# Order of the first loads, split product, shared copies and a halved last tile in a fused linear-attention and mixer kernel

## Chip, cores, metric

One core of a Trainium2 chip. The metric is the device time of one execution in microseconds (us).

In the lines of the profile PE is TensorE (PEld its loads of weights), DVE VectorE, ACT ScalarE, POOL GpSimd and SP SyncE; a "bank" is a buffer in PSUM, into which PE writes. A line of the chain (the work that ended last, followed back step by step) gives its start in us from the start of the span, its length in us, and what ran; L363 is line 363 of that kernel's file. The granted clock is the share of full speed that TensorE was given, 1.00 being all of it.

## The reference

Linear attention with phi(x) = elu(x) + 1, then an MLP mixer over tokens and channels, for 8 batches, 8 heads, 576 tokens, head size 64:

```python
q_p, k_p = phi(q), phi(k)
kv = einsum('bhsd,bhse->bhde', k_p, v);  z = sum(k_p, axis=2)
x = einsum('bhsd,bhde->bhse', q_p, kv) / (einsum('bhsd,bhd->bhs', q_p, z)[..., None] + 1e-6)
# x laid out as (batch, 576, 512)
h = relu(x.T @ w_tok1) @ w_tok2;   u = x + h.T        # token mixing, 256 wide
out = u + relu(u @ w_ch1) @ w_ch2                     # channel mixing, 1536 wide
```

## The kernel before

Matmuls run in bf16. The channel matmuls of a batch are interleaved with the attention of a later one, so PE is busy nearly all the time. Only the first batch has nothing to hide behind; it has code of its own, in two groups of four heads ("group 0" and "group 1", index `c`). For the first batch phi(k) is held as two terms that are summed in the product: `kr` = relu(k) and `kp` = min(exp(k), 1).

```python
for c, nms in enumerate(("kq", "qk")):        # SyncE's queue: k0, q0, q1, k1
    for nm in nms:
        load(nm, 0, c)
...
for c in range(2):                            # GpSimd's queue: v of group 0, v of group 1
    load_v0(c)
...
warm(27)                                      # matmuls on the identity, result unused
...
ksum_first(0, act)                            # sums of k: 18 matmuls, copies on ScalarE
warm(2)
kv_first(0, act)                              # product k by v: 36 matmuls, 64 rows each
...
nd_first(0)                                   # denominators, numerators
...
ksum_first(1, act); kv_first(1, act)
num_first(0, 0, R); num_first(0, R, 1)
nd_first(1)
mm1_first(...)                                # token matmul 1
mm2_first(0, [0, 1]); mm2_first(0, [2, 3])    # token matmul 2 in tiles of 64 columns,
mm2_first(1, [0, 1])                          #   each with u = x + h on VectorE
utr_first([0, 1], act)                        # transposes of u, copy of 128x1024 on ScalarE
mm2_first(1, [2, 3])
mm3(0, 0, range(0, 2))                        # channel matmul 1, first column
utr_first([2], act); utr_first([3], dve)
for mc in range(1, 3): mm3(0, mc, range(0, 2))   # "second column" below: mc = 1
```

The 64 rows of each batch that do not fill a tile of 128 ("tail rows") are transposed in pairs by a DMA into `uTt`, and `m3t` are the channel matmuls on them. The last batch ends with one output tile whose 12 matmuls of 512 columns are followed by one add and two stores:

```python
def mm4_end(p, t):
    ...
    nc.vector.tensor_tensor(out=o, in0=ps, in1=u[b][:, r, :], op=ALU.add)
    ... # the two halves of the partitions are stored from SyncE and from ScalarE
for n in range(2, B):
    ...
    big = m3(n) + m3t + m4(p, [4, 5, 6, 7, 8] if n + 1 < B else [8, 4, 5, 6, 7])
```

## Time and profile before

| | before |
|---|---|
| median time, 3 runs | 267.51 us (267.28 to 267.62) |
| span of the profiled execution | 265.8 us |
| PE busy | 256.6 us, 97% |
| second column of channel matmuls starts | 23.17 us |
| PE's last matmuls end (chain) | 261.13 us |
| last store lands | 264.51 us |

The time is the span plus about 1.8 us. The profile's lines of the opening and of the end stand in the prediction. "Second column" is the mark at which the opening is over: from there on PE has almost no gap. It is read from the timeline as the start of the second run of channel matmuls (the first has two matmuls only). Where PE does not wait, starts of matmuls in the timeline are some 0.04 to 0.2 us ahead of the same matmuls in the chain, which counts from when the result before them was complete.

### The profile page before, as it was taken

The page shows a single profiled execution, that of the slowest core. Times are in us where ns is not written, and L with a number is a line of the kernel's source. Part 1 is how long each engine was busy: PE and PEld are TensorE (multiplying, and loading weights), DVE is VectorE, ACT ScalarE, POOL GpSimd, SP SyncE. Part 2 cuts the span into 40 slices and gives each one's busy share as a digit, 9 for nine tenths or more (in the row PEclk, how much of TensorE's full clock was granted, in tenths as well). Part 3 has the DMA queues.
Part 4 walks back from the last instruction along what each step waited for, and adds up shares of the span by engine and source line. Part 5 has one row for each costly group of instructions (what it writes and reads, how often), then busy time and mean ns, then how long its engine had stood idle before and what let it go on. Part 6 is the DMA issues. An engine that isn't in the chain of part 4 may idle for free.

```text
span 265.8 us, 5142 instructions
## 1 busy us (share of the span) xinstructions
PE 256.6 (97%) x2107; PEld 134.1 (50%) x2107; DVE 158.2 (60%) x311; ACT 132.8 (50%) x200; POOL 33.4 (13%) x54
## 2 busy tenths in 40 slices
PE   7999989999999999999999999999999999999992
PEld 2684445554744454455554554455564554444641
DVE  5764967966839686948684286939684272320121
ACT  5645768268464358525771358435870363036300
POOL 9720300120002300030001300030001300000000
PEclk9999999999999999999999999999999999999999
DMA  7999999399406995899999990671074500730043
GB/s 260 246 203 280 373 214 399 133 191 402 168 2 125 191 383 201 108 239 369 285 411 210 258 409 32 143 171 36 2 135 116 118 2 0 162 94 2 0 118 79
DMA packets 49927, 48.34 MB, mean 182 GB/s; under 512 B 30256, under 2 KB 35248, under 8 KB 49904
## 3 DMA queue, kind: packets, MB, share of 16 engines
q1 hardware_dynamic: 41824, 35.53, 46.8%
q0 software_dynamic: 7440, 11.44, 20.4%
q10 hardware_dynamic: 640, 1.05, 1.2%
q8 instruction: 16, 0.26, 0.4%
q14 instruction: 7, 0.06, 0.1%
HBM read 35.85 MB, written 9.44 MB: 170 GB/s over the span
## 4 chain that ended last, share of the span: by engine, by line
PE 87%; DMA 4%; DVE 3%; ACT 2%; issue 1%; POOL 0%; ACTq 0%; POOLq 0%
PE h_ps L501 34%; PE c_ps L475 27%; PE a_ps L248 5%; PE h_ps L261 5%; DMA uTt<-ut 4%; PE c_ps L489 4%; PE bank L545 3%; PE nd_ps L210 3%; PE kv_ps L169 2%; ACT e L125 1%; PE bank L363 1%; PE bank L413 1%; DVE e L139 1%; DVE vs L151 1%; PE bank L385 1%
## 5 line engine op out<-in xcount | busy, mean ns | idle before, releaser
L482 ACT ACTIVATE cr<-c_ps 128x512 bf16<-128x512 f32 x91 | 53.5, 598 | 78.0 <-PE c_ps L475 77.8
L475 PE MATMUL c_ps<-uT,wc 128*128 128x512 bf16 x384 | 91.5, 379 | 0.4 <-ACT uT L444 0.4
L501 PE MATMUL h_ps<-wc,cr 128*128 128x512 bf16 x384 | 87.4, 379 | 0.0
L501 PEld LDWEIGHTS <-cr 128*128 128x128 bf16 x384 | 37.1, 98 | 43.0
L475 PEld LDWEIGHTS <-wc 128*128 128x128 bf16 x384 | 35.7, 98 | 36.5 <-issue 1.0
L518 DVE TENSOR_TENSOR o_sb<-h_ps,u 128x512 f32<-128x512 f32 x32 | 21.8, 688 | 28.0 <-PE h_ps L501 27.9
L523 POOL DMA_DIRECT2D out_dram<-o_sb x24 | 14.9, 627 | 154.1 <-DVE o_sb L518 154.1
L222 DVE TENSOR_TENSOR x<-nd_ps,den 128x512 bf16<-128x512 f32 (+1 forms) x42 | 25.3, 602 | 1.4
L139 DVE TENSOR_SCALAR e<-e 128x1152 bf16<-128x1152 bf16 x30 | 13.9, 463 | 12.7 <-ACT e L125 12.6
L125 ACT ACTIVATE e<-k_raw 128x1152 bf16<-128x1152 f32 x16 | 18.7, 1170 | 2.3 <-DMA k_raw<-in_k_dram 2.3
L125 ACT ACTIVATE e<-q_raw 128x1152 bf16<-128x1152 f32 x16 | 18.5, 1161 | 1.6 <-DMA q_raw<-in_q_dram 1.4
L273 DVE TENSOR_TENSOR u<-h_ps,x 128x1024 bf16<-128x1024 f32 x12 | 14.4, 1219 | 7.2 <-PE h_ps L261 7.1
L219 DVE TENSOR_SCALAR den<-nd_ps 128x8 f32<-128x8 f32 (+1 forms) x42 | 6.8, 163 | 19.2 <-PE nd_ps L210 18.6
L261 PE MATMUL h_ps<-ar,w2p 128*128 128x512 bf16 x60 | 16.0, 379 | 0.1
L210 PEld LDWEIGHTS <-qT 128*128 128x128 bf16 x140 | 11.4, 98 | 9.3 <-issue 0.2
L210 PE MATMUL nd_ps<-kvbd,qT 128*128 128x130 bf16 x140 | 15.1, 223 | 0.0
L248 PE MATMUL a_ps<-x,w 128*128 128x512 bf16 x56 | 14.4, 379 | 0.0
L151 ACT CAST vs<-v_raw 128x1152 bf16<-128x1152 f32 x12 | 13.9, 1160 | 0.0
L528 DVE TENSOR_TENSOR o_sb<-h_ps,ut 128x512 f32<-128x512 f32 x4 | 2.8, 690 | 18.7 <-PE h_ps L501 18.7
L251 ACT ACTIVATE ar<-a_ps 128x512 bf16<-128x512 f32 x14 | 7.6, 595 | 12.1 <-PE a_ps L248 12.1
L140 DVE TENSOR_TENSOR qp<-e,y 128x1152 bf16<-128x1152 bf16 x16 | 12.1, 758 | 0.6
L131 DVE TENSOR_SCALAR y<-q_raw 128x1152 bf16<-128x1152 f32 x16 | 12.1, 756 | 0.3
(102 smaller groups left out, 218.1 us busy)
## 6 DMA issues: line engine op xcount, KB each, us to landing
k_raw<-in_k_dram SPq DMA_DIRECT2D x16, 576.0 KB, 9.0
q_raw<-in_q_dram SPq DMA_DIRECT2D x16, 576.0 KB, 7.0
v_raw<-in_v_dram SPq DMA_DIRECT2D x14, 576.0 KB, 11.0
out_dram<-o_sb POOLq DMA_DIRECT2D x24, 256.0 KB, 4.7
wc<-in_moe_w_ch_dram POOLq DMA_DIRECT2D x8, 384.0 KB, 9.8
out_dram<-o_sb SPq DMA_DIRECT2D x10, 128.0 KB, 2.3
out_dram<-o_sb ACTq DMA_DIRECT2D x8, 128.0 KB, 2.6
out_dram<-o_sb POOLq DMA_DIRECT2D x6, 128.0 KB, 7.0
```

The lines of the kernel that those rows point to most:

```text
L125: nc.scalar.activation(out=e, in_=f, func=AF.Exp)
L139: nc.vector.tensor_scalar(out=e, in0=e, scalar1=1.0, scalar2=None, op0=ALU.min)
L151: copy(out=vs[:, js, :, 0:D], in_=raw["v", n % 2][:, js].rearrange("p j (t d) -> p j t d", t=T))
L210: nc.tensor.matmul(out=o[:, a], lhsT=qT[b][:, t0:t0 + 128], rhs=kvbd[b][:, c, a], start=True, stop=True)
L222: nc.vector.tensor_tensor(out=x[b][:, rs[0]:rs[0] + m, HG * D * g:HG * D * (g + 1)].rearrange("p r (h d) -> p r h d", h=HG), in0=v_[:, :, ...
L248: nc.tensor.matmul(out=ps[:, mt], lhsT=w1t[:, b, ms] if r == R else w1[:, r, ms], rhs=x[b][:, r, :], start=(r == 0), stop=(r == R))
L261: nc.tensor.matmul(out=ps[:, i], lhsT=w2v(kt, r, b), rhs=ar[b][:, kt, :], start=(kt == 0), stop=(kt == NT - 1 and not add))
L475: nc.tensor.matmul(out=ps, lhsT=wc1[:, kj, 128 * mc:128 * mc + 128], rhs=uT[b][:, :, kj], start=(kj == 0), stop=(kj == NDM - 1))
L482: nc.scalar.activation(out=cr[b][:, mc, :], in_=ps, func=AF.Relu)
L501: nc.tensor.matmul(out=ps, lhsT=crt[:, kc, :] if t == 8 else cr[b][:, kc, 128 * r:128 * r + 128], rhs=wc2[:, kc, :], start=(kc == 0), stop ...
L518: nc.vector.tensor_tensor(out=o, in0=ps, in1=u[b][:, r, :], op=ALU.add)
L523: (nc.scalar if last and e else put).dma_start(out=outv[2 * p + b, :, 2 * r0 + e:2 * r0 + e + 2 * m - 1:2], in_=live["o"][half[e], 0:m])
```

## The change

Its intent: bring v of group 0 forward by taking k of group 1 out of SyncE's queue; shorten the warm-up, since PE can start earlier; start group 1's product with relu(k), which is ready before the other term; keep PE occupied in the wait with four matmuls on the identity ("fillers"); let ScalarE and VectorE share copies and additions of the u stage; make what follows PE's last matmul shorter.

```diff
-    for c, nms in enumerate(("kq", "qk")):
-        for nm in nms:
-            load(nm, 0, c)
+    for nm, c in (("k", 0), ("q", 0), ("q", 1)):
+        load(nm, 0, c)
...
-    for c in range(2):
-        load_v0(c)
+    load_v0(0)
+    load("k", 0, 1, put=nc.gpsimd)
+    load_v0(1)
...
-    warm(27)
+    warm(19)
...
-    nd_first(0)
+    nd_first_den(0)
+    nd_first_num(0)
+    for _ in range(4):
+        nc.tensor.matmul(out=live["last"][:, HG * D:2 * HG * D], lhsT=identity,
+                         rhs=identity[:, None, :].to_broadcast([128, 2, 128]), start=True, stop=True)
...
-    ksum_first(1, act)
-    kv_first(1, act)
+    kv_first(1, (kr,))
+    ksum_first(1, (kr,))
+    ksum_first(1, (kp,))
+    kput_first(1, act)
+    kv_first(1, (kp,))
+    kvput_first(1, act)
...
-    mm2_first(1, [0, 1])
-    utr_first([0, 1], act)
+    mm2_first(1, [0, 1], True)
     mm2_first(1, [2, 3])
+    utr_first([0], act)
+    utr_first([1], dve)
...
 def mm2_first(c, rs, add=False):
+            if add:                                   # x is added by PE, then copied by ScalarE
+                nc.tensor.matmul(out=ps[:, i], lhsT=identity, rhs=x[0][:, r, cs],
+                                 start=True, stop=False)
...
-            big = m3(n) + m3t + m4(p, [4, 5, 6, 7, 8] if n + 1 < B else [8, 4, 5, 6, 7])
+            big = m3(n) + m3t + m4(p, [4, 5, 6, 7, 8])
+            if n + 1 == B:
+                big = m3(n) + m3t + m4(p, [8, 4, 5, 6]) + [lambda: mm4_last(0), lambda: mm4_last(1)]
```

`mm4_last(c)` makes 12 matmuls of 256 columns for one half of the columns of the last tile, adds and stores that half. The copies of group 0's product also move from ScalarE to VectorE.

More of the change, by code (lines that the diff above doesn't have):

```diff
@@ L107, in after, with load @@
         return ins
-    def load(nm, n, c, gate=None):
+    def load(nm, n, c, gate=None, put=nc.sync):
         src_ = src[nm][n].rearrange("(j a) (p t) d -> (a p) j (t d)", a=2, t=T)
         js = slice(2 * c, 2 * c + 2)
-        return after(nc.sync.dma_start(out=raw[nm, n % 2][:, js], in_=src_[:, js]), gate)
+        return after(put.dma_start(out=raw[nm, n % 2][:, js], in_=src_[:, js]), gate)
     def load_v0(c):
@@ L346, in qput_first, with ksum_first, kput_first, kv_first @@
         qtr_put(0, c, TS[h], live["qtr", c][h], put, qT[c])
-    def ksum_first(c, copy):
-        ps = bank()[:, 0:2]
-        for k_ in (kr, kp):
+    def ksum_first(c, terms):
+        if kr in terms:
+            live["ks"] = bank()[:, 0:2]
+        for k_ in terms:
             for t in range(T):
-                nc.tensor.matmul(out=ps, lhsT=k_[:, c, t].rearrange("p i d -> p (i d)"),
+                nc.tensor.matmul(out=live["ks"], lhsT=k_[:, c, t].rearrange("p i d -> p (i d)"),
                                  rhs=ones, start=(k_ is kr and t == 0),
                                  stop=(k_ is kp and t == T - 1))
+    def kput_first(c, copy):
         for i in range(2):
-            copy(out=kvbd[0][half[i], c, :, (i + 1) * D1 - 1], in_=ps[half[i]])
-    def kv_first(c, copy):
-        ps = sm_tile()[:, :, 0:2 * D]
-        for k_ in (kr, kp):
+            copy(out=kvbd[0][half[i], c, :, (i + 1) * D1 - 1], in_=live["ks"][half[i]])
+    def kv_first(c, terms):
+        if kr in terms:
+            live["kv"] = sm_tile()[:, :, 0:2 * D]
+        for k_ in terms:
             for t in range(T):
                 for a in range(2):
-                    nc.tensor.matmul(out=ps[:, a], lhsT=k_[half[a], c, t],
+                    nc.tensor.matmul(out=live["kv"][:, a], lhsT=k_[half[a], c, t],
                                      rhs=v0[half[a], 2 * c:2 * c + 2, t],
                                      start=(k_ is kr and t == 0), stop=(k_ is kp and t == T - 1))
+    def kvput_first(c, copy):
         for i in range(2):
             copy(out=kvbd[0][half[i], c, :, i * D1:(i + 1) * D1 - 1],
-                 in_=ps[half[i], :, i * D:(i + 1) * D])
+                 in_=live["kv"][half[i], :, i * D:(i + 1) * D])
     def q_cols(r, a, c):
@@ L372, in q_cols, with nd_first_den @@
         return qT[c][:, t0:t0 + 128]
-    def nd_first(c):
+    def nd_first_den(c):
         dn = bank()[:, 0:4 * R1].rearrange("p (r i a) -> p r i a", r=R1, i=2)
@@ L379, in nd_first, with nd_first_num @@
                                  rhs=kvbd[0][:, c, a, D::D1], start=True, stop=True)
+        live["dn", c] = dn, work.tile([128, R1, HG], FP32, name="den0", tag="den0")
+    def nd_first_num(c):
         full = sm_tile().rearrange("p b (r h d) -> p (b r) h d", r=2, h=HG)
-        last = bank()[:, 0:HG * D].rearrange("p (r h d) -> p r h d", r=1, h=HG)
+        live["last"] = bank()
+        last = live["last"][:, 0:HG * D].rearrange("p (r h d) -> p r h d", r=1, h=HG)
         for r in range(R1):
@@ L388, in nd_first @@
                     start=True, stop=True)
-        den = work.tile([128, R1, HG], FP32, name="den0", tag="den0")
-        live["nd0", c] = dn, den, full, last
+        live["nd0", c] = full, last
     def den_first(c):
-        dn, den, _, _ = live["nd0", c]
+        dn, den = live["dn", c]
         nc.vector.tensor_scalar(out=den, in0=dn.rearrange("p r i a -> p r (i a)"),
@@ L398, in num_first @@
     def num_first(c, r0, m):
-        _, den, full, last = live["nd0", c]
+        den = live["dn", c][1]
+        full, last = live["nd0", c]
         nc.vector.tensor_tensor(
@@ L403, in num_first, with mm1_first @@
             in1=den[:, r0:r0 + m, :, None].to_broadcast([128, m, HG, D]), op=ALU.mult)
-    def mm1_first(c, rs):
-        if rs[0] == 0:
+    def mm1_first(c, rs, mts=range(NT)):
+        if rs[0] == 0 and mts[0] == 0:
             live["mm1", c] = sm_tile()[:, :, 0:DM // 2] if c else bank().rearrange(
@@ L409, in mm1_first @@
         ps = live["mm1", c]
-        for mt in range(NT):
+        for mt in mts:
             ms = slice(128 * mt, 128 * mt + 128)
@@ L414, in mm1_first, with mm2_first @@
                                  rhs=x[0][:, r, COLS[c]], start=(r == 0), stop=(r == R))
-        if rs[-1] == R:
+        if rs[-1] == R and mts[-1] == NT - 1:
             nc.scalar.activation(out=ar[0][:, :, COLS[c]], in_=ps, func=AF.Relu)
-    def mm2_first(c, rs):
+    def mm2_first(c, rs, add=False):
         cs = COLS[c]
@@ L424, in mm2_first @@
                     nc.tensor.matmul(out=ps[half[e], i], lhsT=w2r[:, kt, :, 2 * r + e],
-                                     rhs=ar[0][:, kt, cs], start=(kt == 0), stop=(kt == NT - 1))
-        nc.vector.tensor_tensor(out=u[0][:, rs[0]:rs[0] + 2, cs], in0=ps,
-                                in1=x[0][:, rs[0]:rs[0] + 2, cs], op=ALU.add)
+                                     rhs=ar[0][:, kt, cs], start=(kt == 0 and not add),
+                                     stop=(kt == NT - 1))
+        if add:
+            nc.scalar.copy(out=u[0][:, rs[0]:rs[0] + 2, cs], in_=ps)
+        else:
+            nc.vector.tensor_tensor(out=u[0][:, rs[0]:rs[0] + 2, cs], in0=ps,
+                                    in1=x[0][:, rs[0]:rs[0] + 2, cs], op=ALU.add)
     def mm2_first_tail():
@@ L530, in mm4_end, with mm4_last @@
                 put.dma_start(out=outv[2 * p + b, :, 2 * R], in_=o[half[b]])
+    def mm4_last(c):
+        p, b, r, cs = B // 2 - 1, 1, R - 1, COLS[c]
+        ps = ps_big.tile([128, 512], FP32, name="h2_ps", tag="big")[:, 0:DM // 2]
+        for kc in range(NCH):
+            nc.tensor.matmul(out=ps, lhsT=cr[b][:, kc, 128 * r:128 * r + 128],
+                             rhs=wc2[:, kc, cs], start=(kc == 0), stop=(kc == NCH - 1))
+        o = outp.tile([128, 2, DM], FP32, name="o_sb", tag="o_sb")[:, 0, 0:DM // 2]
+        nc.vector.tensor_tensor(out=o, in0=ps, in1=u[b][:, r, cs], op=ALU.add)
+        for e in range(2):
+            (nc.scalar if e else nc.sync).dma_start(out=outv[2 * p + b, :, 2 * r + e, cs],
+                                                    in_=o[half[e]])
     def prep_k(n, g, copy=nc.scalar.copy):
@@ L605 @@
     qput_first(0, 1, act)
-    ksum_first(0, act)
+    ksum_first(0, (kr, kp))
+    kput_first(0, act)
+    warm(2)
+    kv_first(0, (kr, kp))
+    kvput_first(0, dve)
     e_first("k", 1)
-    warm(2)
-    kv_first(0, act)
     k_first(1, 0)
     qtr_first(1)
+    nd_first_den(0)
[3 more added lines that the diff above has]
+                         rhs=identity[:, None, :].to_broadcast([128, 2, 128]), start=True, stop=True)
     k_first(1, 1)
-    nd_first(0)
     den_first(0)
@@ L616 @@
     qput_first(1, 1, act)
-    ksum_first(1, act)
-    kv_first(1, act)
+    kv_first(1, (kr,))
[4 more added lines that the diff above has]
+    kvput_first(1, act)
     num_first(0, 0, R)
     num_first(0, R, 1)
-    nd_first(1)
+    nd_first_den(1)
+    nd_first_num(1)
     mm1_first(0, range(R1))
```

## The prediction

> **What bounds the kernel now.** I read the page first: its busy row, its clock row, and the chain that ended last. Then I read the timeline of the first 26 us and of the last 20 us, the DMA issues with their landings, and the list of what PE waited for.
>
> ```profile
> PE 256.6 (97%) x2107; PEld 134.1 (50%) x2107; DVE 158.2 (60%) x311; ACT 132.8 (50%) x200; POOL 33.4 (13%) x54
> ...
> PE 87%; DMA 4%; DVE 3%; ACT 2%; issue 1%; POOL 0%; ACTq 0%; POOLq 0%
> ```
>
> PE is busy for 97% of the span and carries 87% of the chain. The profile has no other long stage to win from: all that the change can touch is the opening, up to the first full row of the channel matmuls (23.2 us), and the last output tile. What the opening loses or wins should shift everything behind it, because from 23.2 us on PE works nearly without a break. The chain of the opening, in order of time:
>
> ```profile
> 1.36 8.21 PE bank L545 x27
> 9.56 0.50 PE bank L180 x9
> 10.06 0.43 PE bank L352 x18
> 10.49 0.46 PE bank L545 x2
> 10.95 1.14 PE bank L363 x36
> 12.09 0.61 PE bank L180 x9
> ...
> 15.39 0.28 ACT kvbd L367
> ...
> 15.71 0.74 PE bank L385 x10
> 16.45 2.18 PE bank L413 x20
> ```
>
> L545 are matmuls on the identity whose result nobody reads. The first 27 run to 9.57, though the q that the transposes (L180) need is ready sooner: the timeline has its last DVE operation (L140) at 7.58 for 0.76, so 8.34. This cost is hidden: behind it stands the group-0 product k by v (L363), which needs the first half of v. Of the two v issues on GpSimd's queue, at 3.73 and 4.58 us, the first took 7.1 us to land, so 10.87, and L363 starts at 10.9. The two further L545 only fill that wait. The opening is therefore paced by v up to 10.9, by PE's own work to 15.1, then by the eviction of the second product and again by PE.
>
> Why v is late shows in the DMA queues. The first view is the window 5 to 7.5 us, the second 7.75 to 9.5:
>
> ```profile
> q1 hardware_dynamic: 452, 0.98, 103.0%
> ```
> ```profile
> q0 software_dynamic: 227, 0.26, 86.7%
> q1 hardware_dynamic: 96, 0.18, 29.9%
> ```
>
> q1 is SyncE's queue with k0, q0, q1, k1 (the number is the group); q0 is GpSimd's. Up to 7.5 us not one packet of v moves although its issue ended at 4.58, and the engines are full. v starts at about 7.8, when k1, the last of SyncE's four, is nearly through. Landings (issue plus the time to landing): k0 4.5, q0 5.9, q1 8.0, k1 9.8, v0 10.9, v1 12.3. k1 is not even used at 9.8: ScalarE reads it at 11.0.
>
> **What the Trainium skill says.** "DMA: Bandwidth & Descriptors", section "Issuing engines are not separate DMA queues": transfers of all three issuers run on the same 16 engines. So moving k1 to GpSimd adds no bandwidth; it only reorders, which the shares above support (the engines are full before and after 7.75). The same page, "Queues, rings and completion order", says that an engine takes turns between the queues by packets; the first window disagrees, with all packets from q1 while v was waiting. I go by the measurement. "TensorE: Matmul & The Clock Gate", section "Back-to-back issue gap", gives N / 2.4 + 2.5 ns for N columns; the 20 matmuls of 256 columns above take 2.18 us, 109 ns each, which agrees. The same page, section "What's actually happening": full clock after some 3.4 us of sustained work. The trace agrees in kind: the warm-up matmuls are 0.43 us apart up to 5.9 us, and 0.215 after. Nineteen of them still pass that point.
>
> **The change, part by part.**
>
> *Warm-up 27 to 19.* 8 x 0.215 = 1.7 us less, so they end at 7.85 instead of 9.57. The transposes of q then start when q is ready, 8.35, and take 0.7; the sums of k (L352) 0.43; the two fillers 0.43: PE reaches the first product at 9.95.
>
> *k1 behind v0 on GpSimd's queue.* If v0 takes the place in which k1 stood, it starts when q1 is nearly through, at 7.8 less one transfer (256 packets of 2304 bytes at some 170 per us, 1.5 us): 6.3. With the 3.0 us it took from start to landing before, it lands at about 9.35. k1 follows 1.5 later, 10.85; v1 stays at 12.3, as the bytes ahead of it are the same. q1 may land 0.3 later, 8.3, which nobody feels, as VectorE evicts a transposed q until 9.6. So the first product starts at 9.95 and not 10.91: **0.96 us earlier**, and PE is now the limit there.
>
> *Four fillers of 256 columns* behind the group-0 numerator: 4 x 0.109 = **0.44 us back**. They are meant for the wait on k1. Does PE wait there? From 9.95: product 1.13, transposes 0.65, denominator 0.24, numerator 0.6 (its eviction, now two DVE copies of some 0.25 as an estimate between the 0.18 of 128x20 and 0.41 of 128x256, is ready at 11.7): 12.55. k1 at 10.85 gives relu(k1) on VectorE from 11.7 to 12.5, and v1 lands at 12.3. So there is hardly a wait to fill, and the fillers are on the path: group 1's product starts at 13.0.
>
> *Product of group 1 by terms.* PE does the same 36 + 18 matmuls, in an order in which relu(k1) goes first. exp(k1) runs 10.85 to 12.0, its minimum on VectorE 12.6 to 13.05; PE asks for it at 13.8. So no wait: the product ends at 14.55 against 15.09, eviction 0.54 and numerator 0.74 as before, to 15.9 against 16.45. **Net to here 0.5 us.** Token matmul 1 (L413, 2.18 us) is PE-bound before and after.
>
> *u and copies.* Before, from the start of token matmul 2 at 18.56 to the second column of channel matmuls at 23.3: 4.74 us, with PE idle 0.66 of 4.55. Three DVE adds of 0.65 in a row, then one ScalarE copy of 128x1024 (1.01) stand in it. After: 32 matmuls at 0.07 plus two identity ones at 0.11 give 2.46; eight transposes of which the first four end 0.3 later; ScalarE copies 128x512 (0.59) beside VectorE (0.42) instead of 1.01; 0.43 of channel matmul and 0.55 of transposes follow. Counting 0.2 from PE's last matmul to its reader, 2.46 + 0.3 + 0.2 + 0.6 + 0.03 + 0.43 + 0.55 = 4.57. **0.17 us won.** The shorter copy is partly paid with the identity matmuls and with the fourth product standing before the transposes.
>
> *Last tile in halves.* PE 24 x 0.109 = 2.62 against 12 x 0.216 = 2.59. VectorE's add shrinks from 0.69 (128x512) to 0.42 (the 128x256 of L222 or L400). The stores behind it are half as large, but on an idle queue they took 2.3 to 2.6 us for any of the last eight, mostly not data; I give them 0.05. The chain's end:
>
> ```profile
> 248.16 12.96 PE h_ps L501 x60
> 261.13 0.02 issue
> 261.15 0.69 DVE o_sb L518
> ```
>
> **0.3 us won**, sure, since nothing runs beside it.
>
> Sum: 0.5 + 0.17 + 0.3 = 1.0 us. 267.51 - 1.0 = **266.5**.
>
> **Rivals.** (1) v0's late start is GpSimd's own latency and not k1's place. Its first issue at 3.73 moves nothing for 4.1 us; the stores later in the kernel, on a calm queue, land 3 us after issue. Then v0 starts at 7.8 as before, lands at 10.4 as it no longer shares, k1 at 11.9 and v1 at 13.1; the fillers eat the 0.45 won, and only u and the tail remain: 267.0. For it speaks the 4.1; against it that v starts just as SyncE's packets run out, and that in 28 to 31 us GpSimd's queue gets 39 packets against SyncE's 526. (2) k1 lands over 1.2 us later than I say, at 12.1 or more. Then its exponential, the minimum and the second half of the product become the bound, and each further us costs one: at 13 the kernel is at 267.4. For it: nothing shows a k load on GpSimd's queue. (3) PE stands still at 7.9 to 8.35 and waits on transposes and copies after; if the clock falls, the opening's 6 us of PE work could stretch by 1 to 2: 268. Against it: the gap is short, and before, gaps of 0.3 to 0.4 at 15.4 and 21.9 left the clock at 1.00. (4) Everything earlier meets a later bound: the channel weights land at 17.8 and 19.7, the later quarters by 26.5, well ahead of use; the transposed tail at 131.6 arrives as PE asks for it, but its queue moves with PE. I expect the shift to carry through.
>
> **Range and chances.** Rivals 1 and 2 put some weight at 267.0 to 267.4; a v0 that lands early with a k1 early enough, and a larger gain in the u stage (all of its 0.66 idle is there to win), put some at 265.7. So 265.7 to 267.3. Faster by 2% means under 262.2, five times my sum, and there is not that much idle PE in the opening; slower by 2% needs a lost clock and more.
>
> **What would show it.** In the changed profile: v0's landing at 9.3 to 9.6 with k1 at about 10.9, and the first product at 9.95 (rival 1: 10.4 or later); PE without idle time before the group-1 product, with the fillers at 12.5; the group-1 numerator done at 15.9; the second column of channel matmuls from 22.6; a last add of 0.42, and from PE's last matmul to the end of the span 4.35 instead of 4.67. It is wrong if PE waits for relu(k1) or the minimum of k1, if the clock row has a step in the first 20 us, or if the time saved by 23 us is not found at 248 us.

## The result

The changed kernel took 267.17 us (median of 4 runs, 266.86 to 267.82) against 267.39 (266.95 to 267.62) for the kernel before: ratio 0.9997, 95% interval 0.9974 to 1.002. Ratios here are the mean time of one kernel's fast runs over the mean of the other's in the same rounds, so not quite the ratio of the medians. In a second measurement it was 0.9979 (0.9966 to 0.9992), that is 0.6 us less. The forecast gain of 1.0 us is not there: the two results are 0.1 and 0.6 us, and only the second is clear of zero.

The page of the changed kernel has the same busy row, as far as such a small change could show:

```profile
PE 256.5 (97%) x2117; PEld 135.2 (51%) x2117; DVE 159.0 (60%) x314; ACT 132.2 (50%) x199; POOL 33.7 (13%) x55
```

The queues in the window 5 to 7.5 us of the changed kernel:

```profile
q1 hardware_dynamic: 333, 0.70, 75.8%
q0 software_dynamic: 115, 0.13, 30.8%
```

Before, q0 (GpSimd's) had no packet there. v of group 0 lands at 9.67 instead of 10.87, and the chain of the opening reads:

```profile
8.50 0.68 PE bank L180 x9
...
9.61 0.45 PE bank L575 x2
10.06 1.11 PE bank L367 x36
...
12.62 0.45 PE bank L647 x4
13.07 0.10 issue
13.17 0.68 PE bank L367 x18
13.85 0.54 PE bank L353 x18
14.38 0.63 PE bank L367 x18
...
15.62 0.74 PE bank L395 x10
```

L367 is the product, L647 the fillers, L353 the sums, L395 the numerator. The first product is 0.9 us earlier than before; group 1's numerator only 0.09 (15.62 against 15.71). Next, the u stage, the chain of the kernel before and then of the changed one:

```profile
18.63 0.68 PE bank L424 x8
...
21.23 1.02 ACT uT L444
...
22.29 0.59 PE c_ps L475 x2
...
23.33 2.16 PE c_ps L475 x10
```
```profile
18.54 1.14 PE bank L437 x14
19.69 0.21 PE bank L433
19.90 0.44 PE bank L437 x4
20.34 0.21 PE bank L433
20.55 0.90 PE bank L437 x11
...
21.82 0.59 ACT uT L461
...
23.50 2.16 PE c_ps L492 x10
```

The stage starts 0.09 us earlier and ends 0.17 later (23.50 against 23.33; by starts of matmuls 23.33 against 23.17). So the opening as a whole came out 0.16 later and not 0.67 earlier. One pair says little about so small a difference: the old opening reached the second column at 23.17, 23.30 and 23.39 in its three traces (before, `tail_only`, `before_row_later`), the changed one at 23.33, 23.05 and 23.48 (changed, `tail_whole`, `after_again`), on average 23.29 both. The u stage alone takes the same in every trace: 4.61 us from the start of token matmul 2 in those three, 4.86 in these three. The 0.16 us of the pair are not seen at the end either, for the kernel before had a wait at 131 us that the changed one had for a smaller part:

```profile
119.69 11.95 DMA uTt<-ut
131.64 0.04 issue
131.68 1.05 PE c_ps L489 x16
```

This is the chain of the kernel before: PE has nothing to do until the transposed tail rows land at 131.64. In the changed kernel they land at 131.64 too, while PE comes later. PE's end in the chain is 261.16 against 261.13. What remains is the tail:

```profile
258.53 2.63 PE h_ps L554 x24
261.16 0.02 issue
261.19 0.42 DVE o_sb L557
```

The add takes 0.42 instead of 0.69, and the last stores, issued at 261.64, land at 263.86: 2.22 us, against 2.64 before. The span ends at 265.1 instead of 265.8.

### The profile page after: what moved, and what is told of

It is laid out like the page before. It is cut to its first block, busy times and chain, and to the rows that moved or that the text cites. A ratio compares the mean times of both kernels' runs of the same rounds, so it can differ in the third digit from the quotient of the medians.

```text
span 265.1 us, 5171 instructions
## 1 busy us (share of the span) xinstructions
PE 256.5 (97%) x2117; PEld 135.2 (51%) x2117; DVE 159.0 (60%) x314; ACT 132.2 (50%) x199; POOL 33.7 (13%) x55
## 4 chain that ended last, share of the span: by engine, by line
PE 87%; DVE 6%; ACT 2%; DMA 1%; issue 1%; ACTq 0%
PE h_ps L518 34%; PE c_ps L492 27%; PE a_ps L248 6%; PE h_ps L261 5%; PE c_ps L506 4%; PE nd_ps L210 3%; PE kv_ps L169 2%; DMA k_raw<-in_k_dram 1%; DVE y L131 1%; DVE e L139 1%; PE h_ps L554 1%; PE bank L437 1%; DVE cr L496 1%; PE bank L367 1%; ACT e L125 1%
## 5 line engine op out<-in xcount | busy, mean ns | idle before, releaser
L518 PE MATMUL h_ps<-wc,cr 128*128 128x512 bf16 x372 | 84.8, 379 | 0.0
L518 PEld LDWEIGHTS <-cr 128*128 128x128 bf16 x372 | 36.0, 98 | 41.6
L492 PEld LDWEIGHTS <-wc 128*128 128x128 bf16 x384 | 35.8, 98 | 36.5 <-issue 1.2
L535 DVE TENSOR_TENSOR o_sb<-h_ps,u 128x512 f32<-128x512 f32 x31 | 21.1, 688 | 26.1 <-PE h_ps L518 26.0
L210 PEld LDWEIGHTS <-qT 128*128 128x128 bf16 x140 | 11.4, 98 | 9.3 <-issue 0.2
L210 PE MATMUL nd_ps<-kvbd,qT 128*128 128x130 bf16 x140 | 15.1, 223 | 0.0
```

The lines of the kernel that those rows point to most:

```text
L210: nc.tensor.matmul(out=o[:, a], lhsT=qT[b][:, t0:t0 + 128], rhs=kvbd[b][:, c, a], start=True, stop=True)
L492: nc.tensor.matmul(out=ps, lhsT=wc1[:, kj, 128 * mc:128 * mc + 128], rhs=uT[b][:, :, kj], start=(kj == 0), stop=(kj == NDM - 1))
L518: nc.tensor.matmul(out=ps, lhsT=crt[:, kc, :] if t == 8 else cr[b][:, kc, 128 * r:128 * r + 128], rhs=wc2[:, kc, :], start=(kc == 0), stop ...
```

## The experiments

Theory A: the opening wins nothing, because the identity matmuls of the u stage cost four times what I counted and group 1 waits for v; the tail wins 0.7; the wait for the tail rows decides what of an opening reaches the end. Theory B: my account, with the opening carried one to one. Each kernel ran five rounds beside the kernel before; those of one group of four ran on one chip. All results were correct.

**The tail alone** (`tail_only`): the kernel before with the last line of the diff and `mm4_last`.

> The kernel before with only the last row tile in column halves. Theory A (the tail is worth what the profiles show: span 265.8 to 265.1, the last landing 0.42 us and the last add 0.27 us shorter, and the rest of the change gives nothing): 0.6 to 0.7 us faster than before, PE's last matmul at 261.1 to 261.2 as before, last landing about 2.7 us after it. Theory B (my prediction: only the add is shorter, 0.3 us, and the stores' landing hardly depends on their size): 0.3 us faster.

266.85 us against 267.66, ratio 0.9974 (0.9959 to 0.9989): 0.7 us. PE's last step ends 0.1 us earlier than before, and the last landing follows the start of the last matmul by 2.98 us against 3.78. The trace decides for A: 0.11 us of the 0.80 are the shorter last matmul, 0.27 the add, 0.42 the stores. The time alone would not, as B's 0.3 us stands at the edge of its interval. The tail is worth twice what I gave it.

**The opening alone** (`tail_whole`): the changed kernel with

```diff
-                big = m3(n) + m3t + m4(p, [8, 4, 5, 6]) + [lambda: mm4_last(0), lambda: mm4_last(1)]
+                big = m3(n) + m3t + m4(p, [8, 4, 5, 6, 7])
```

> The changed kernel without the halves in the last tile, so the opening's part of the change alone. Theory A (the opening is 0.16 us later at the second column of channel matmuls, and a wait for the transposed tail rows at 131.6 us absorbs it): the same as before within 0.1 us, second column at 23.3 against 23.2. Theory B (what happens in the opening shifts the end one to one): 0.16 us slower than before.

267.52 against 267.66, ratio 1.0005 (0.9988 to 1.0022): the same. In this execution the second half of v landed at 12.38 instead of 13.04, group 1's product started at 12.89 instead of 13.17 and the second column at 23.05; then PE stood 0.29 us in front of the tail rows. So A's result is met, its mark of 23.3 is not: the mark varies with the landing of v. B is not refuted by the time, as a loss of 0.16 us is a ratio of 1.0006, inside the interval.

**The u stage as before** (`u_before`):

```diff
-    mm2_first(1, [0, 1], True)
+    mm2_first(1, [0, 1])
+    utr_first([0, 1], act)
     mm2_first(1, [2, 3])
-    utr_first([0], act)
-    utr_first([1], dve)
```

> The changed kernel with the u stage and its copies as they were before. Theory A (the identity matmuls cost 0.42 us each instead of 0.11, because the array has to change between 128 and 64 columns): the stretch from the first matmul of token matmul 2 to the second column of channel matmuls is 4.6 us as before and not 4.86, so 23.1 instead of 23.33; in the time 0.25 us faster than the changed kernel if openings carry through (0.45 to 0.6 us under the kernel before with the tail), or no faster if the wait at 131.6 takes it. My prediction's account says that this is slower by 0.17 us.

266.78 us, ratio 0.9974 (0.996 to 0.9988). From the start of token matmul 2 at 18.31 to the second column at 22.92 it is 4.61, as A says; my account, under which this should lose, falls. The time is that of the tail alone: the opening won here waits 0.32 us for the tail rows.

**Identity matmuls of 64 columns** (`identity_halves`):

```diff
-                nc.tensor.matmul(out=ps[:, i], lhsT=identity, rhs=x[0][:, r, cs],
-                                 start=True, stop=False)
+                for e in range(2):
+                    nc.tensor.matmul(out=ps[half[e], i], lhsT=identity[:, half[e]],
+                                     rhs=x[0][:, r, cs], start=True, stop=False)
```

> The changed kernel with each identity matmul of the u stage cut into two of 64 columns, the form of its neighbours. Theory A (the cost lies in changing between 128 and 64 columns): the four products with their additions take 2.2 to 2.4 us instead of 2.92, and the second column of channel matmuls starts 0.4 to 0.5 us earlier, at 22.8 to 22.9. Rival (the identity matmuls are slow for another reason, such as the wait for a bank or for x): the products stay at 2.8 us or more.

266.20 us, ratio 0.9953 (0.9938 to 0.9968), 1.3 us less than before. The chain of its u stage:

```profile
18.44 1.15 PE bank L438 x14
19.58 0.11 PE bank L434 x2
19.69 0.23 PE bank L438 x4
19.92 0.11 PE bank L434 x2
20.03 0.70 PE bank L438 x12
```

Line by line against the changed kernel: the additions 0.11 each instead of 0.21, the four matmuls between them 0.23 instead of 0.44, the last group 0.70 instead of 0.90. Nothing changed in the groups of 4 and 12; they got shorter because their neighbours now have their form. The four products take 2.29 us (18.44 to 20.73) instead of 2.92; so they do in all three traces with the halved identity, against 2.90 to 2.92 in the seven with the whole one. The reason is shown: a change between 128 and 64 columns costs, on the way in and on the way out, and not the identity as such. This agrees with the Trainium skill, "TensorEngine Tiling (Array Packing)", section "Key Properties": "Mode switching requires drain".

**The change again** (`after_again`), unaltered.

> The changed kernel unaltered, against the kernel before on the chip of the runs below, because its first four times scatter by a whole us. If the parts add up (the tail alone 0.26% faster, the opening alone the same within 0.17%): 0.15 to 0.35% faster, 0.4 to 0.9 us. If the first figure was right and something in the whole undoes the tail: under 0.1%.

267.10 against 267.68, ratio 0.9979, that is 0.6 us: it fits the sum of the parts (tail 0.7 us less, opening the same within 0.1 or so).

**Product in one piece, no fillers** (`kv_whole_no_fillers`):

```diff
-    (the four fillers)
-    kv_first(1, (kr,))
-    ksum_first(1, (kr,))
-    ksum_first(1, (kp,))
+    ksum_first(1, (kr, kp))
     kput_first(1, act)
-    kv_first(1, (kp,))
+    kv_first(1, (kr, kp))
```

> The changed kernel with the product of group 1 in one piece after its sums, as before, and without the four fillers. Theory A (the fillers stand mostly in a wait for k1 and the second half of v, and the split by terms adds changes between 64 and 128 rows): PE waits for relu(k1) and its minimum until 12.7 to 13.0 us, does the sums in the wait for v, and the group-1 numerator starts at 15.2 to 15.4 instead of 15.62; 0.2 to 0.4 us faster than the changed kernel. Rival (fillers and terms are worth what they were made for: the clock or the overlap): the numerator starts at 15.6 or later, no gain or a loss.

266.85, ratio 0.9977 (0.9958 to 0.9996): no difference from the changed kernel. The numerator started at 15.76, so A's 15.2 to 15.4 is a miss and the rival is right in this: undoing the split by terms and the fillers together wins nothing. The sums could not start before 13.43. The profile names a copy of the transposed q on ScalarE as their releaser: by the code's order of banks the sums take over its PSUM bank, and ScalarE makes it after exp(k1). This execution lost another 1.44 us in front of the tail rows, which landed at 133.1.

**k of group 1 back on SyncE** (`k1_on_sync`):

```diff
-    for nm, c in (("k", 0), ("q", 0), ("q", 1)):
+    for nm, c in (("k", 0), ("q", 0), ("q", 1), ("k", 1)):
...
-    load("k", 0, 1, put=nc.gpsimd)
```

> The changed kernel with k of group 1 as SyncE's fourth load, as before. Theory A (v waits for the last of SyncE's loads): the first half of v lands at 10.8 to 11.0, the first product starts at 10.9 to 11.0 instead of 10.0, and with the fillers still in place the group-1 numerator starts at 16.0 to 16.4 instead of 15.62, 0.3 to 0.7 us slower than the changed kernel. Rival (GpSimd's own latency): v at 9.7 as in the changed kernel.

268.05, ratio 1.0014 (0.999 to 1.0038), against 0.9979 for the changed kernel in the same rounds: 0.9 us more. The queue window 5 to 7.5 us:

```profile
q1 hardware_dynamic: 455, 0.98, 103.2%
```

No packet of v, which lands at 11.32; the product starts at 11.37. The first packet on GpSimd's queue moves at 7.80; it does so at 7.80 to 7.90 in all four traces with k1 in SyncE's queue, at 7.83 in the kernel before, and at 6.47 to 6.59 in all ten without. So v waits for SyncE's loads, as the prediction had it, and not for a latency of GpSimd. v came 0.3 to 0.5 us later than expected, and the numerator, at 16.81, with it.

**All of it** (`all_identity_halves`): the 64-column identity, no fillers, product in one piece.

> The changed kernel with identity matmuls of 64 columns, without the fillers and with group 1's product in one piece: the best version that the readings so far point to. Theory A: second column of channel matmuls at 22.2 to 22.5, against 22.6 with the halved identity alone; in the time 0 to 0.3 us faster than that, as the wait for the transposed tail rows at 131 us may take the rest: 0.45 to 0.6% faster than before.

A miss: 267.23 with runs from 266.05 to 269.13, ratio 0.999 (0.9959 to 1.002). In the profiled execution the clock fell to half from 16.15 to 19.56 us, and token matmul 1 took 3.62 us (16.83 to 20.45) instead of 2.27. The second column started at 24.68. Two more of the six runs, 267.77 and 268.06, had a low mean clock too (0.992 and 0.991); the other three took 266.05 to 266.69.

**Tail rows later, on three kernels.** For the second pair of batches (n = 3):

```diff
             big = m3(n) + m3t + m4(p, [4, 5, 6, 7, 8])
+            if n == 3:
+                big = m3(n) + m4(p, [4, 5]) + m3t + m4(p, [6, 7, 8])
```

> The kernel before, with one thing moved in the third pair's middle: the channel matmuls on the transposed tail rows (the ones that wait for their transfer at 131.6 us) come after two of the output tiles, so the wait has 5.2 us of other matmuls in front. Theory A (this wait cuts off what the opening wins, and its varying end is a good part of the scatter): PE's gap in front of these matmuls is gone, PE's last matmul starts 0.2 to 0.4 us earlier, 0.1% faster than before, and the runs lie closer together. Theory B (the wait is an accident of reading): no change, or a loss because ScalarE now evicts them behind other work.

`before_row_later`: 267.57 against 267.70, ratio 0.9997 (0.9981 to 1.0014). The gap is gone and PE's last matmul starts 0.04 us earlier although this execution's second column was 0.22 later (23.39); in the time there is no gain. Of A only the missing gap is met, not its 0.2 to 0.4 us.

> The changed kernel with the same move. Theory A: no gap in front of these matmuls, 0.1 to 0.3 us faster than the changed kernel, so 0.25 to 0.4% faster than before. Theory B: as the changed kernel, 0.2%.

`after_row_later`: 266.56, ratio 0.9977 (0.9951 to 1.0003), not told apart from the changed kernel. Its profiled run (268.75) was one with the clock at half from 15.99 to 19.40, fillers or not: v had landed at 13.41, and the timeline has PE idle for 0.61 us behind the fillers.

> The changed kernel with the 64-column identity matmuls and with the same move: the best version so far. Theory A: the 0.55 to 0.7 us that the halves win in the opening all reach the end, 0.45 to 0.65% faster than before with little scatter. Theory B: 0.4% with the scatter of the others.

`halves_row_later`, with the 64-column identity: 265.95 us (265.95 to 266.21), ratio 0.9944 (0.993 to 0.9958), 1.5 us less than before. It is the fastest, with the least scatter; that it is better than `identity_halves` is not shown, as the intervals overlap.

**No fillers** (`no_fillers`), the product still by terms:

```diff
-    for _ in range(4):
-        nc.tensor.matmul(out=live["last"][:, HG * D:2 * HG * D], lhsT=identity, ...)
```

> The changed kernel without the four fillers, the product still by terms. Theory A (they stand in a wait for v and cost nothing, but without them the gap of 0.6 us or more lowers the clock in some executions, as in one trace without fillers at 16.2 to 19.6 us): the product of group 1 starts when the second half of v lands, as with fillers, the median within 0.1% of the changed kernel, but single runs 1 to 2 us longer. My prediction's account (they are on the path): 0.3 to 0.4 us faster in all runs.

266.77, ratio 0.997 (0.9955 to 0.9985), one run of 268.58. The product started at 13.21, with the fillers at 13.17 in the changed kernel, each time just behind the landing of v, so there they stand in a wait, as A says. Where v lands earlier they do not. The first two lines are from the chain of `no_fillers`, the last two from that of `tail_whole`, where v had landed at 12.38 and the product follows the fillers (L647) without a gap:

```profile
5.38 7.70 DMA cr<-in_v_dram
...
13.21 0.68 PE bank L367 x18
```
```profile
12.52 0.44 PE bank L647 x4
12.95 0.61 PE bank L367 x18
```

The run of 268.58 was profiled; two of its stretches (columns: start and end, length, then busy time of PE, PEld, DVE, ACT, POOL, then the granted clock, the DMA share and GB/s):

```profile
12.14:15.55 3.41, 2.53 (x71) 2.09 (x69) 3.04 (x7) 2.27 (x7) 2.69 (x4) 1.00 1.31 202
15.55:18.96 3.41, 3.30 (x21) 2.63 (x21) 1.95 (x5) 0.06 (x1) 0.00 (x0) 0.50 1.32 203
```

A stretch of 3.41 us with PE busy for 2.53, then one of the same length at half clock. Such a stretch lowers the mean clock of a run by 0.006. A mean of 0.994 or less is on record for 4 of 19 runs without fillers (three of them of `all_identity_halves`) and for 1 of 44 with them. This count was made afterwards and rests on five runs: that the fillers keep the clock up is a hint, not shown.

### One account for all traces

Take the start of the second column, PE's end (start of the last matmul plus one step, 0.216 us for 512 columns or 0.109 for 256), and the wait for the tail rows (the step into the first of these matmuls beyond 0.216):

| kernel | second column | wait | PE's end | end - column - wait |
|---|---|---|---|---|
| before | 23.17 | 0.29 | 260.95 | 237.49 |
| changed | 23.33 | 0.11 | 260.99 | 237.55 |
| tail_only | 23.30 | 0 | 260.84 | 237.54 |
| tail_whole | 23.05 | 0.29 | 260.85 | 237.51 |
| u_before | 22.92 | 0.32 | 260.77 | 237.53 |
| identity_halves | 22.61 | 0 | 260.15 | 237.54 |
| after_again | 23.48 | 0.15 | 261.17 | 237.54 |
| kv_whole_no_fillers | 23.48 | 1.44 | 262.45 | 237.53 |
| k1_on_sync | 24.52 | 0.86 | 262.91 | 237.53 |
| all_identity_halves | 24.68 | 0.50 | 263.26 | 238.08 |
| before_row_later | 23.39 | 0 | 260.91 | 237.52 |
| after_row_later | 25.32 | 0 | 262.87 | 237.55 |
| halves_row_later | 22.49 | 0 | 260.03 | 237.54 |
| no_fillers | 24.93 | 0.18 | 262.65 | 237.54 |

In 13 of 14 traces the rest of the kernel takes 237.49 to 237.55 us. The opening does shift everything behind it one to one, but for one wait, of 0 to 1.4 us. The exception, `all_identity_halves`, has 0.55 us more. Set beside `identity_halves`, 0.40 of it is a second wait for a transfer: the matmuls of a later batch's numerators (L210) stop after the first until a transposed q lands at 121.5, 6.88 us after its issue. Another 0.15 is lost at 36.5 in a wait of PE for VectorE's q.

## Why the prediction was wrong

It added 0.5, 0.17 and 0.3 us. In the profiled pair these came out as 0.09, -0.25 and 0.7. The first varies with the landing of v: token matmul 2 starts at 18.56 to 18.78 in the three traces of the old opening and at 18.19 to 18.62 in the six of the changed one at full clock (those with all its parts up to there), on average 18.68 and 18.37. So about 0.3 of the 0.5 was there, and the u stage took 0.25 of it back.

- **Right: v and k1.** The mechanism holds. v lands at 9.67 (8.89 to 9.84 in the traces with that order) for 9.35, k1 at 11.07 for 10.85, the first product starts at 9.99 for 9.95. Rival 1 is refuted by `k1_on_sync`. The warm-up ended at 8.27 and not at 7.85, because its slow pace lasted to 6.8 us instead of 5.9; this cost nothing, as q was ready at 8.45 only.
- **Failed: "v1 stays at 12.3, as the bytes ahead of it are the same".** It landed at 13.04, and between 12.38 and 13.41 in the others. In five traces PE began group 1's product 0.13 to 0.14 us after that landing (changed, `after_again`, `u_before`, `no_fillers`, `after_row_later`); in `after_again` the profile's chain names the minimum of k1, which ended at nearly the same time, but the product does not need it: in `u_before` it started at 13.00 and the minimum ended at 13.07. I worked out a place in the queue and gave it no scatter.
- **Failed in the pair: fillers "on the path".** They stand in this wait; in `no_fillers`, where v landed at 13.07, the product started no sooner. In the three traces in which v landed at 12.38 to 12.79 (`tail_whole`, `halves_row_later`, `identity_halves`) they were on the path, as I had it, and the product started at 12.89 to 13.07 for my 13.0. So it hangs on v. Whether they are worth having is not shown: medians with and without are alike, and a clock that falls was seen without them and, once, in `after_row_later`, with them.
- **Mis-sized: the product by terms, "ends at 14.55".** The step from its start to the eviction took 1.86 us (13.17 to 15.04, before rounding). I had used 1.56, chain durations laid onto starts; by the same measure the kernel before takes 1.74 (13.38 to 15.12). The other 0.12 I put down to two more changes between 64 and 128 rows, which I had left out: in `kv_whole_no_fillers`, without the split, the step is 1.74 again (13.43 to 15.17). No run separates the changes of form from the rest of the order.
- **Failed, the largest single term: "two identity ones at 0.11" in the u stage.** 4.86 us instead of 4.57, and 4.61 before. My 4.74 for before was wrong too: it runs from a start in the timeline (18.56) to one in the chain (23.3), so by one measure my own sum won 0.04 and not 0.17. Two matmuls of 128 columns in the midst of 64-column ones cost 0.63 us more than the same additions in 64 columns (2.92 against 2.29). With that alone mended, the gain is the 1.0 that I had forecast and a little more (`identity_halves`, 0.9953), but from other parts: the tail gives 0.7 of it. That the sums agree is luck.
- **Mis-sized: the tail, 0.3.** The add gave its 0.27; the stores gave 0.42 and not 0.05. I had taken "2.3 to 2.6 us for any of the last eight" for a fixed cost although all eight had the same size, so this says nothing of how it depends on size.
- **Half right: "I expect the shift to carry through".** It does, up to the wait for the tail rows. I saw that these rows arrive as PE asks for them, and then took it that they move with PE; in the pair before and after they landed at 131.64 both times, with openings 0.16 apart. Over all 14 traces they landed 107.9 to 109.6 us after the second column: they move with the opening, but with a scatter as large as the gains at stake.
- **Rival 3, the clock,** was named and given no weight. It did not touch the changed kernel's profiled run. It is one reason for single long executions: three profiled ones, 268.58 to 269.13, have a stretch at half clock. It is not the only one: `k1_on_sync` had a run of 269.42 with a mean clock of 0.998, and `kv_whole_no_fillers` lost its 1.44 us at full clock.

## What to carry to other kernels

An instruction's cost can depend on its neighbours (an addition took 0.21 us here, and 0.11 in the form of the matmuls beside it): before you give PE an extra matmul of another tile form, look at the groups beside it, and give it their form. Where a change is worth a few tenths, find each wait behind it that ends with a transfer and not with the engine's own work: such a wait can take a gain and hide a loss, and the medians alone will not tell which. And do not call a transfer's time fixed from transfers that all have one size.

## What the Trainium skill lacked or had wrong

- "DMA: Bandwidth & Descriptors", section "Queues, rings and completion order": an engine takes turns between queues at packet granularity. Here GpSimd's queue got 0 packets against SyncE's 452 in 5 to 7.5 us, though the issue of its transfer was over, and 39 against 526 in 28 to 31 us; with one load less in SyncE's queue it got 115 against 333 in 5 to 7.5 us. As its first packet then moved at 6.58 instead of 7.83, the transfer was ready for at least 1.25 us in which it got no turn.
- "TensorEngine Tiling (Array Packing)", section "Key Properties", says that a change of mode drains the engine, but not what that costs: here 0.31 us for each 128-column matmul between 64-column ones (half of 2.92 - 2.29).
- "TensorE: Matmul & The Clock Gate", section "What's actually happening": the clock falls after an idle window of some 3.4 us. In three traces it fell after 3.41 us in which PE was busy for 2.30 to 2.54; in one (`kv_whole_no_fillers`) it stayed up after such a stretch with 2.49. So PE need not be idle for a whole window. The same page, section "A second HAM failure mode: psum-queue depth-cycling", has the clock fall under frequent short gaps too, but no page gives the busy share at which it falls, and these traces do not settle it.
- No page has measured times of stores by their size for this chip. Here, at the end of the kernel: 2.64 us from issue to landing for two stores of 128 KB, 2.22 for two of 64 KB.
